# Opening of a fused block: engine orders written out, first block's tokens before the value weights' scale, first x tiles loaded first

## The chip, the cores and the metric

The kernel runs on one core of a Trainium2 chip. The metric is the device time of one execution in microseconds (us); lower is better. The engines are PE (TensorE: matrix products and transpositions), DVE (VectorE), ACT (ScalarE), POOL (GpSimd) and SP (SyncE, which issues nearly all DMAs here). Each works through its own queue in order and waits on semaphores of the others.

## The reference

The block is an attention layer followed by a mixture of 4096 small experts with product keys, each behind a layer norm, for 2048 tokens of 448 features, 16 heads. The change touches only the attention's projections:

```python
def _A_ref(x, wqkv, wo):              # x: layernorm(A_x), (1, 2048, 448)
    qkv = (x @ wqkv).reshape(B, S, 3, H, Dh).transpose(2, 0, 3, 1, 4)
    q, k, v = qkv[0], qkv[1], qkv[2]
    scores = jnp.einsum("bhqd,bhkd->bhqk", q, k) * (Dh ** -0.5)
    p = _softmax(scores, axis=-1)
    o = jnp.einsum("bhqk,bhkd->bhqd", p, v)
    return o.transpose(0, 2, 1, 3).reshape(B, S, D) @ wo
x = A_x
h = x + _A_ref(_layernorm(x), A_wqkv, A_wo)
return h + _B_ref(_layernorm(h), ...)
```

## The kernel before

The program has three parts: the projections to queries, keys and values (`qkv`, the first 154 us), attention woven with preparations of the experts, and the experts. The opening is the start of the first part. It works on blocks of 512 tokens (four blocks, `b`), each of four tiles of 128 tokens (`j`).

Every float32 product is made of three float16 products: an operand is split into a high and a low float16 part (`products`, eleven PE rows for the 448 features: four high x high, four high x low, three low x high; the last 64 features' low part sits in the free half of the fourth high tile, which `lows` patches in with its second instruction).

Weights must be scaled by a power of two first. `Scale` does that: `see` reduces each weight tile to a maximum per partition (DVE, line 141), `spread` reduces these and spreads the result over a 128x128 tile `every` (lines 144 and 145), PE transposes it (line 149), and `set` makes the maximum over all partitions and from it the scale in four small dependent steps (lines 161 to 164). `scaled` then has ACT write the high parts (`wqkh`, `wvh`, line 355) and DVE the low parts (`wqkl`, `wvl`, line 356). `scale_wqk(g)` does it for the key and query weights of head group `g` (two tiles `wqkr`), `scale_wv` for the value weights (two tiles `wr`).

`normed(b)` normalizes a block: statistics per tile (lines 393 and 394), the reciprocal root on POOL (`rsqrt`, lines 109 and 112), the normalization itself into one of two buffers `xn` (line 115), four PE transpositions into one of two PSUM buffers `tr` (line 121), ACT's copy to the high part `XH` (line 96), and DVE's low part `XL` and patch of `XH` (lines 127 and 128).

`keys(0, b)` projects a block to keys (`proj`, PE line 92 into `pq`), squares and copies them on ACT (lines 429 and 431), stores both halves, sums the squares on PE (line 434) and keeps a maximum. `values_of(b)` projects the block's four tiles to values (44 PE rows, line 92) and scales them on ACT (line 416).

`qkv` runs under a scheduler that orders PE, DVE, ACT and SP by itself; only POOL's order is the program's. The code's order there is `scale_wqk(0)`, `normed(0)`, `scale_wv()`, `normed(1)`, and then block by block keys and values. All loads are issued by SP: constants `ct`, two `wqkr`, four tiles of x, two `wr`, then the next x tiles, the next weights and, ahead of need, weights of the later parts.

## Time and profile before

| what | value |
|---|---|
| median of 3 runs | 1644.02 us (1638.12, 1644.02, 1646.05) |
| profiled execution | 1642.62 us, of which the span from first to last instruction is 1640.8 us |
| busy share of the span | PE 95%, DVE 73%, ACT 57%, POOL 22% |
| mean granted PE clock | 0.987 |
| PE waits longest in the first 40 us | 8.2 us for `every`, 6.6 us for `xn` (four times), 2.0 us for the weight scale |

The profile is a record of one execution. The sum of busy times tells which engine is full over the whole span; the windows tell it stage by stage, and the timeline shows each engine's instructions with their start, their length and, in brackets, the idle time before them and what ended it. Rows of equal instructions are merged (x8), so that a row's length is that of the group.

### The profile page before, as it was taken

To read this page: it belongs to the slowest core of one execution; us is meant where nothing else is said; L and a number is where in the kernel's file an instruction comes from. 1 tells how busy PE (TensorE), PEld (TensorE's weight loads), DVE (VectorE), ACT (ScalarE), POOL (GpSimd) and SP (SyncE) were. 2 spreads that over 40 slices of the span, in tenths; PEclk is the share of its full clock that TensorE was granted. 3 is DMA by queue.
4 is the path that set the end of the run, shared out by engine and by line. 5 is a ranking of instruction groups with operands and counts; after the bars stand their busy time and mean duration, and the time that the engine had idled before them with its cause. 6 is when DMAs were issued, how large, how long until landed. Compare 5 with 4: busy or idle time off the path is not lost.

```text
span 1640.8 us, 33316 instructions
## 1 busy us (share of the span) xinstructions
PE 1560.6 (95%) x12585; PEld 678.9 (41%) x12585; DVE 1198.4 (73%) x3875; ACT 931.9 (57%) x1272; POOL 364.7 (22%) x488
## 2 busy tenths in 40 slices
PE   5999999999999998999988998999999999999999
PEld 3444222233333332233325654455545554555444
DVE  7762432645688677765798999959999899779832
ACT  3545778979888887888773443233423344334322
POOL 1241003555204565487524000000000000000000
PEclk9999999999999999999998999999999999999999
DMA  8424965677853475457622434444444533554454
GB/s 281 134 97 129 305 215 190 213 242 253 286 173 96 151 242 180 130 162 235 189 87 78 131 94 148 125 125 144 119 127 138 156 105 108 156 153 129 117 146 129
DMA packets 158881, 263.34 MB, mean 160 GB/s; under 512 B 14336, under 2 KB 90880, under 8 KB 158720
## 3 DMA queue, kind: packets, MB, share of 16 engines
q1 hardware_dynamic: 154496, 259.12, 50.5%
q10 hardware_dynamic: 4224, 2.10, 0.4%
q8 instruction: 98, 1.61, 0.4%
q14 instruction: 63, 0.52, 0.1%
HBM read 211.88 MB, written 49.28 MB: 159 GB/s over the span
## 4 chain that ended last, share of the span: by engine, by line
PE 63%; DVE 27%; DMA 5%; ACT 2%; issue 2%; POOL 1%; SPq 0%; DVEq 0%; POOLq 0%; ACTq 0%
PE acc L1190 14%; PE M L92 12%; PE A L589 10%; PE S L563 9%; PE A L92 7%; PE pq L92 6%; DVE p L969 4%; DVE ti L799 3%; DVE pos L826 2%; DVE G L990 2%; DVE ti L798 2%; ACT P L567 2%; DVE fg L954 2%; DMA raw<-in_uT_dram 2%; PE M L262 1%
## 5 line engine op out<-in xcount | busy, mean ns | idle before, releaser
L567 ACT ACTIVATE P<-S,escale 128x1024 f32<-128x1024 f32 x512 | 534.5, 1131 | 75.9 <-PE S L563 75.9
L1190 PE MATMUL acc<-v,w 128*128 128x448 f16 x1536 | 305.4, 352 | 0.1
L589 PE MATMUL A<-P,V 128*32 128x512 f32 x2048 | 266.0, 609 | 3.7 <-DVE o L594 3.7
L563 PE MATMUL S<-qS,kS 32*128 32x512 f16 x3072 | 240.1, 380 | 7.7 <-ACT P L567 6.0
L1190 PEld LDWEIGHTS <-w 128*128 128x128 f16 x1536 | 148.7, 98 | 141.3 <-ACT w L1164 0.9
L1164 ACT ACTIVATE w<-ring 128x512 f16<-128x512 f32 x128 | 80.5, 630 | 209.7 <-PE acc L1190 109.9
L92 PEld LDWEIGHTS <-u 128*128 128x128 f16 x1408 | 133.7, 98 | 152.5 <-issue 12.3
L969 DVE TENSOR_TENSOR p<-st,iota 128x2048 f16<-128x2048 f16 x128 | 156.0, 1219 | 7.7 <-PE A L996 4.1
L563 PEld LDWEIGHTS <-kS 32*128 32x128 f16 x3072 | 65.8, 92 | 210.6 <-issue 171.7
L92 PE MATMUL A<-XHb,u 128*128 128x512 f16 x568 | 137.8, 386 | 5.1 <-DVE G L990 3.9
L1165 DVE SCALAR_TENSOR_TENSOR w<-w,ring 128x512 f16<-128x512 f16 x128 | 87.2, 687 | 66.2 <-ACT w L1164 66.2
L92 PE MATMUL M<-w,XHb 128*128 128x512 f16 x512 | 127.9, 380 | 4.2 <-DVE ob L580 3.1
L1163 DVE SCALAR_TENSOR_TENSOR ring<-ring,wscale,G 128x512 f32<-128x512 f32 x128 | 92.7, 744 | 34.6 <-ACT ring L1149 34.5
L92 PE MATMUL M<-XHb,u 128*128 128x512 f16 x456 | 112.4, 382 | 0.8 <-DVE G L990 0.8
L1149 ACT ACTIVATE ring<-A,ugelu 128x512 f32<-128x512 f32 x71 | 48.5, 684 | 84.6 <-PE A L92 84.6
L589 PEld LDWEIGHTS A<-P,V 128*32 128x32 f32 x2048 | 45.8, 109 | 119.1 <-issue 108.3
L850 POOL TENSOR_TENSOR sel<-sel,iv 128x256 f16<-128x256 f16 x80 | 54.4, 712 | 171.6 <-DVE sel L846 171.6
L798 DVE MAX8 ti<-fresh 128x8 f32<-128x64 f32 x384 | 80.6, 210 | 16.3 <-ACT fresh L776 16.2
L1149 ACT ACTIVATE ring<-M,ugelu 128x512 f32<-128x512 f32 x57 | 39.2, 688 | 81.7 <-PE M L92 81.5
L799 DVE FIND_INDEX8 ti<-ti,fresh 128x8 uint32<-128x64 f32 x384 | 84.2, 219 | 0.0
L1026 POOL TENSOR_SCALAR raw<-raw,scale 128x512 f32<-128x512 f32 (+1 forms) x64 | 47.3, 740 | 151.8 <-PE M L262 112.2
L954 DVE TENSOR_TENSOR fg<-f,st 128x2048 f16<-128x2048 f16 x64 | 78.0, 1218 | 0.1
(197 smaller groups left out, 2130.4 us busy)
## 6 DMA issues: line engine op xcount, KB each, us to landing
v<-vs SPq DMA_DIRECT2D x128, 336.0 KB, 2.9
u<-us SPq DMA_DIRECT2D x128, 256.0 KB, 2.6
w<-wp SPq DMA_DIRECT2D x56, 512.0 KB, 5.9
kS<-ks SPq DMA_DIRECT2D x64, 256.0 KB, 4.5
V<-vd SPq DMA_DIRECT2D x64, 256.0 KB, 2.8
raw<-in_uT_dram SPq DMA_DIRECT2D x64, 256.0 KB, 5.3
wr<-in_wq_dram SPq DMA_DIRECT2D x32, 448.0 KB, 4.3
raw<-in_v_dram SPq DMA_DIRECT2D x64, 224.0 KB, 5.1
```

Of the source, the lines that this page charges most:

```text
L92: nc.tensor.matmul(ps, l, r, start=i == 0, stop=i == len(pairs) - 1)
L563: nc.tensor.matmul(S[j // 2][:, j % 2], kS[r, a, 128 * (k % 4):128 * (k % 4) + 128], qS[r, c], start=m == 0, stop=m == 2)
L567: nc.scalar.activation(Pt[:, 2 * i:2 * i + 2], S[i], AF.Exp, scale=escale[:, n % 4:n % 4 + 1])
L589: nc.tensor.matmul(O[n][32 * j:32 * j + 32], V[:, k % 4, j], Pt[:, j], start=k == 0, stop=k == NT - 1)
L798: nc.vector.max(t8[:, 4 * i + k], src[:, 64 * k:64 * k + 64])
L799: nc.vector.max_index(i8[:, 4 * i + k], t8[:, 4 * i + k], src[:, 64 * k:64 * k + 64])
L954: nc.vector.tensor_tensor(fg.rearrange("p t k f u -> p t k (f u)"), f1.rearrange("p t f u -> p t (f u)").unsqueeze(2).to_broadcast([128, T ...
L969: newest[0] = nc.vector.tensor_tensor(p1, pairs(0, s, TG, 128), ids(TG, 128), op=OP.is_equal).ins
L1149: nc.scalar.activation(act, p, AF.Gelu_apprx_tanh, scale=ugelu)
L1163: nc.vector.scalar_tensor_tensor(av, av, wscale, of_expert(b, f), op0=OP.mult, op1=OP.mult)
L1165: nc.vector.scalar_tensor_tensor(w[:, 1], w[:, 0], -LS, a, op0=OP.mult, op1=OP.add)
L1190: nc.tensor.matmul(acc[j][:, :D], l, r, start=f == 0 and k == 0, stop=f == 31 and k == 2)
```

## The change

No operation is added or removed. Three things move.

The loads: the first two tiles of x are issued before the constants and the first key and query weights, the other two behind them.

The order of the opening: `scaled` and the two scale functions become generators that stop after each step, `normed` is cut into the methods of `Tokens`, and a new function `opening` calls the steps one by one, with the engines PE, DVE and ACT bound to the order in which they are written. It holds the first weights' scale, all of block 0's normalization, the first key product, the value weights' scale and the key rows' end. The scheduler may still put other work (statistics of later blocks, reductions of later weights) between these steps. `values_of(0)` then comes before `normed(1)`, not behind the keys.

The diff, cut to its core:

```diff
-        nc.sync.dma_start(ct, cst)
+        load_x(0, (0, 1))
+        nc.sync.dma_start(ct, cst)
         fetch_wqk(0)
-        load_x(0)
+        load_x(0, (2, 3))
...
             S.spread()
+            yield
             S.set(S.turned(ps, "tr")[:, 0])
+            yield
             for wr, (hi, low) in zip(raws, parts):
                 nc.scalar.activation(hi, wr, AF.Identity, scale=S.scale)
+                yield
                 nc.vector.scalar_tensor_tensor(low, wr, S.scale, hi, op0=OP.mult, op1=OP.subtract)
+                yield
...
+        class Tokens:
...
+            def stats(self, j, n=1):
+                nc.vector.bn_stats(self.st[:, j], self.xt[:, j])
+                nc.vector.bn_aggr(self.mv[:, j], self.st[:, j])
+                if n:
+                    rsqrt(self.rstd[:, j + 1 - n:j + 1], self.mv[:, j + 1 - n:j + 1, 1], n, XS)
+            def high(self, j):
+                xn = wk.tile([128, D], F32, name="xn")
+                norm(self.xt[:, j], xn, self.mv[:, j, 0:1], self.rstd[:, j:j + 1], nc.vector)
+                self.pt[j] = ps.tile([128, 4, 128], F32, name="tr")
+                turn(self.pt[j], xn)
+                copy(nc.scalar, XH[self.b][:, :, 128 * j:128 * j + 128], self.pt[j])
+            def low(self, j):
+                c = slice(128 * j, 128 * j + 128)
+                lows(XH[self.b][:, :, c], XL[self.b][:, :, c], self.pt.pop(j))
...
+        def opening():
+            wq, wv = scale_wqk(0), scale_wv()
+            T = Tokens(0)
+            nc.scalar.activation(blk, ct[:, C_BLK:C_BLK + 128], AF.Copy)
+            T.stats(0)
+            T.stats(1)
+            next(wq)
+            T.high(0)
+            T.stats(2)
+            next(wq)
+            next(wq)
+            T.high(1)
+            T.stats(3)
+            T.low(0)
+            T.high(2)
+            T.low(1)
+            T.high(3)
+            next(wq)
+            T.low(2)
+            T.low(3)
+            load_x(2)
+            pk = proj(wqks[0][0], 0)
+            for _ in wq:
+                pass
+            next(wv)
+            next(wv)
+            next(wv)
+            keep_keys(0, 0, pk)
+            for _ in wv:
+                pass
         def qkv():
-            scale_wqk(0)
-            normed(0)
-            scale_wv()
-            nc.scalar.activation(blk, ct[:, C_BLK:C_BLK + 128], AF.Copy)
+            with tc.manual_schedule(engines={ET.PE, ET.DVE, ET.Activation}):
+                opening()
             fetch_wqk(1)
+            values_of(0)
             normed(1)
             for b in range(NB):
                 if b in (1, 2):
                     normed(b + 1)
-                keys(0, b)
-                if b < 2:
+                if b:
+                    keys(0, b)
+                if b == 1:
                     values_of(b)
```

What this makes of the engines' queues is seen at three places. Rows are given as line, operation, output and input; `tops` are the maxima of a weight tile, `top` and `floor` the steps to its scale. First DVE, from the end of block 0's low parts to the spread of the value weights' maximum. Before:

```order
L141 TENSOR_REDUCE tops_331<-wr 128x1
L393 BN_STATS st<-xb 128x6
L127 TENSOR_TENSOR XL_206<-tr,XH_202 128x3x128
L128 TENSOR_TENSOR XH_202<-tr,XH_202 64x128
L144 TENSOR_REDUCE top_332<-tops_331 128x1
L127 TENSOR_TENSOR XL_206<-tr,XH_202 128x3x128
L128 TENSOR_TENSOR XH_202<-tr,XH_202 64x128
L145 COPY every<-top_332 128x128
```

Now:

```order
L127 TENSOR_TENSOR XL_206<-tr,XH_202 128x3x128
L128 TENSOR_TENSOR XH_202<-tr,XH_202 64x128
L360 SCALAR_TENSOR_TENSOR wqkl<-wqkr,scale_262,wqkh 128x512
L373 TENSOR_SCALAR escale<-floor_261 128x1
L141 TENSOR_REDUCE tops_346<-wr 128x1 x2
L404 BN_AGGR mv<-st 128x2
L403 BN_STATS st<-xb 128x6
L144 TENSOR_REDUCE top_347<-tops_346 128x1
L403 BN_STATS st<-xb 128x6
L145 COPY every<-top_347 128x128
```

The first of the two value reductions (`tops` from `wr`) stood further up before, at row 18 of DVE's queue, the second ahead of the last two tiles' low parts; now both stand together behind all low parts and the weights' low part.

Second PE, from the end of the first key product to the first value row. Before:

```order
L92 LDWEIGHTS wqkh
L92 MATMUL pq<-XL_206,wqkh 128x512
L121 MATMUL tr<-ct,xn 128x128 x8
L92 LDWEIGHTS XH_202
L92 MATMUL pq<-wvh,XH_202 128x448
```

Now:

```order
L92 LDWEIGHTS wqkh
L92 MATMUL pq<-XL_206,wqkh 128x512
L149 MATMUL tr<-ct,every 128x128
L92 LDWEIGHTS XH_202
L92 MATMUL pq<-wvh,XH_202 128x448
```

Eight transpositions of block 1 stood between the key product and the values; now the spread of the value weights' maximum stands there, which before came in the middle of the key product.

Third PE, where block 0's values end and block 1's keys begin. Now:

```order
L92 LDWEIGHTS XL_206
L92 MATMUL pq<-wvh,XL_206 128x448
L121 MATMUL tr<-ct,xn 128x128 x16
L92 LDWEIGHTS wqkh
L92 MATMUL pq<-XH_203,wqkh 128x512
L121 MATMUL tr<-ct,xn 128x128 x4
```

Before, the same place read:

```order
L92 LDWEIGHTS XL_206
L92 MATMUL pq<-wvh,XL_206 128x448
L121 MATMUL tr<-ct,xn 128x128 x8
L92 LDWEIGHTS wqkh
L92 MATMUL pq<-XH_203,wqkh 128x512
```

All sixteen transpositions of block 1 now stand in one piece behind the values of block 0; before, they were done by then, and the eight shown were the first of block 2.

More of the change, by code (lines that the diff above doesn't have):

```diff
@@ L473, in qkv @@
                 if g < 3:
-                    scale_wqk(g + 1)
+                    for _ in scale_wqk(g + 1):
+                        pass
                 if g < 2:
```

42 lines of the change are left out of this document (18 added, 24 removed).

## The prediction

> **What bounds the kernel now.** I read the page first: the busy digits of the 40 slices, then the chain that ended last.
>
> ```profile
> PE   5999999999999998999988998999999999999999
> DVE  7762432645688677765798999959999899779832
> ...
> PE 63%; DVE 27%; DMA 5%; ACT 2%; issue 2%; POOL 1%; SPq 0%; DVEq 0%; POOLq 0%; ACTq 0%
> ```
>
> A slice is 41 us. PE is at 9 tenths or more nearly everywhere except in the first, and it holds 63% of the chain, so what the change can win lies in that first slice. Windows of 10 us show how much (busy us of PE follow the first comma):
>
> ```profile
> 0.00:10.00 10.00, 0.47 (x1) 0.18 (x1) 4.11 (x13) 1.59 (x2) 1.91 (x18) 1.00 0.77 236
> 10.00:20.00 10.00, 5.37 (x20) 3.67 (x20) 9.79 (x26) 3.61 (x6) 2.24 (x5) 1.00 0.89 295
> 20.00:30.00 10.00, 7.95 (x43) 4.46 (x43) 9.02 (x26) 4.90 (x8) 1.35 (x3) 1.00 0.84 292
> 30.00:40.00 10.00, 8.70 (x50) 4.68 (x49) 8.84 (x23) 4.00 (x8) 2.23 (x3) 1.00 1.01 296
> 50.00:60.00 10.00, 9.91 (x54) 5.22 (x52) 5.97 (x13) 5.16 (x9) 1.16 (x1) 1.00 0.37 117
> ```
>
> PE idles 9.5, 4.6, 2.1 and 1.3 us in the first four windows, 17.5 in all; from 40 us it works without a break, through to 60. DVE is busy 9.8, 9.0 and 8.8 us of the second to fourth: the opening is a DVE stage, and each PE wait in it ends on a DVE result. The timeline gives the head of it (start, length):
>
> ```profile
> 1.28 1.34 SPq L332 DMA_DIRECT2D wqkr<-in_wqk_dram  x2
> 2.66 2.04 SPq L324 DMA_DIRECT2D xb<-in_x_dram  x4
> ...
> 5.78 1.49 DVE L141 TENSOR_REDUCE tops<-wqkr 128x1 f32<-128x512 f32 x2 [5.78 <-DMA wqkr<-in_wqk_dram]
> ...
> 8.18 0.47 PE L149 MATMUL tr<-ct,every 128*128 128x128 f32 x1 [8.18 <-DVE every L145]
> ...
> 10.08 0.51 DVE L115 TENSOR_SCALAR xn<-xb,mv,rstd 128x448 f32<-128x448 f32 x1
> 10.50 0.15 DVE L164 TENSOR_SCALAR scale<-floor 128x1 int32<-128x1 int32 x1
> ...
> 10.64 1.97 PE L121 MATMUL tr<-ct,xn 128*128 128x128 f32 x8 [1.98 <-DVE scale L164]
> ```
>
> The key/query weights (wqkr) land first and their scale is ready at 10.65; the first normalized tile is finished at 10.6, so both arrive together. These eight transpositions take 0.25 us each; the same eight at 24.43 below take 0.13, so PE is still at half rate here, whatever the clock column of the window 10:20 says (1.00). Next, the middle part:
>
> ```profile
> 8.04 1.15 DVE L393 BATCH_NORM_STATS2 st<-xb 128x6 f32<-128x448 f32 x2
> ...
> 11.17 1.08 DVE L141 TENSOR_REDUCE tops<-wr 128x1 f32<-128x896 f32 x1
> 12.16 1.41 DVE L356 SCALAR_TENSOR_TENSOR wqkl<-wqkr,scale,wqkh 128x512 f16<-128x512 f32 x2
> 13.48 0.56 DVE L127 TENSOR_TENSOR XL<-tr,XH 128x384 f16<-128x384 f32 x1
> 14.05 0.29 DVE L128 TENSOR_TENSOR XH<-tr,XH 64x128 f16<-64x128 f32 x1
> 15.26 0.94 DVE L115 TENSOR_SCALAR xn<-xb,mv,rstd 128x448 f32<-128x448 f32 x2
> 18.54 1.86 PE L92 MATMUL pq<-XH,wqkh 128*128 128x512 f16 x4 [0.69 <-ACT XH L96]
> 21.81 0.81 PE L92 MATMUL pq<-XL,wqkh 128*128 128x512 f16 x3
> 22.27 0.12 DVE L164 TENSOR_SCALAR scale<-floor 128x1 int32<-128x1 int32 x1
> 23.15 1.96 ACT L355 ACTIVATE wvh<-wr,scale 128x896 f16<-128x896 f32 x2
> 24.43 1.06 PE L121 MATMUL tr<-ct,xn 128*128 128x128 f32 x8 [1.81 <-DVE xn L115]
> 25.10 1.08 ACT L96 ACTIVATE XH<-tr 128x512 f16<-128x512 f32 x2
> 25.33 0.92 PE L92 MATMUL pq<-wvh,XH 128*128 128x448 f16 x4
> ```
>
> The key product runs from 18.54 to 22.62. The value scale (wr, wvh) is ready at 22.39, because the first value reduction stood in DVE's queue at 11.17, early, in the shadow of loads and scales. PE idles 1.8 us, does eight transpositions of block 1 and starts the values at 25.33. And the end of the opening:
>
> ```profile
> 35.02 0.73 PE L92 MATMUL pq<-wvh,XL 128*128 128x448 f16 x3
> 36.95 1.06 PE L121 MATMUL tr<-ct,xn 128*128 128x128 f32 x8 [1.20 <-DVE xn L115]
> 37.85 1.03 PE L92 MATMUL pq<-XH,wqkh 128*128 128x512 f16 x4
> ...
> 50.41 1.04 PE L121 MATMUL tr<-ct,xn 128*128 128x128 f32 x8
> ```
>
> The values of block 0 end at 35.75, the key product of block 1 starts at 37.85, and at 50.41 the transpositions of block 3 begin. At that last place the changed program has issued exactly the same set of PE instructions as this one, and from there on the orders of the engines agree. So the whole effect can be read as: when does PE reach that place, 50.41 now? PE has no slack behind it, so a shift there is a shift of the end.
>
> **The change, step by step.** No instruction is removed or added; only order and load order change. I walk the new queues with the durations above.
>
> Loads: SP needs 0.5 us per x tile (four in 2.04) and 0.67 per weight tile. Two x tiles ahead put the two weight loads 1.0 us later. The first lands 4.5 us after its issue now (1.28 to 5.78); taking the same, the new landings are about 6.8 and 7.5 and the two reductions (starts 0.7 apart) end at 8.3 instead of 7.2. The x tiles come long before; their statistics are hidden in DVE's wait.
>
> First tile: it stands directly behind the spread of the maximum, at 8.3 + 0.15 + 0.2 = 8.7, against 10.08: 1.4 us won. PE starts 0.5 later, at 9.3.
>
> Weight scale: its PE spread now stands behind four transpositions (4 x 0.25) and takes 0.47: 10.7. Then a reduction of 0.27 and three dependent small steps, which cost 0.19 each back to back:
>
> ```profile
> 61.84 0.15 DVE L163 TENSOR_SCALAR floor<-top 128x1 int32<-128x1 int32 x1
> 62.03 0.15 DVE L164 TENSOR_SCALAR scale<-floor 128x1 int32<-128x1 int32 x1
> ```
>
> So the scale is ready at 11.5, 0.9 later than now.
>
> First block: between the scale and the last patch DVE has one normalization (0.47), two statistics (0.54 each), four low parts (0.57 + 0.30 each), two more normalizations and one low weight part (0.70): 6.8 us, and about 0.3 of waiting for ACT's fourth copy: 18.6. PE does the fourth tile's transpositions at 15.9 to 16.9, ACT copies it in 0.6, and the key product starts at 17.7 (now 18.54). Its eleven rows take 0.43 each until the clock rises. I keep that at about 21.5, where it rises now: end at 22.2, 0.4 us won. That is all that is left of the head start.
>
> Value scale: both value reductions now stand behind all of this. From 18.6: second low weight part 0.7, two reductions of 1.0, two statistics of block 1 and small steps 1.4, then the spread: 22.9 us. Behind the spread come PE's 0.42, 0.27, and, between the small steps, two more statistics and three aggregates: 25.3. **The value scale is 2.9 us later than now** (22.39). What is late next is ACT's first value part, 1.96 / 2 = 0.98: PE starts the values at 26.4, having waited since 22.2, and without block 1's first eight transpositions, which now fill such a wait.
>
> Values: 44 rows of 0.19 (four in 0.92, of which 0.35 is the last one's length), the row of squares 0.33, and 0.3 of waiting: 35.3. Then all sixteen transpositions of block 1 in a row. Eight take 1.06; the third tile needs a normalization and a buffer that are free only after ACT's copy (0.54) and DVE's low part (0.87): PE idles about 1.5, then 0.35 and, before the product that needs the fourth copy, 0.85. The product starts at 40.1, not 37.85: 2.3 late. Eight transpositions of block 2 that are done by 37.85 now are still to come, 1.06, of which 0.3 to 0.7 replaces idle time that follows now. Place 50.41 is reached at about 53.4: **3 us late**.
>
> Moved work that I cost at nothing: the squares and the key copy on ACT, now behind the first value part (they feed a maximum that is complete only after block 3, far behind), and POOL's reciprocal roots, which run while DVE is at the weight reductions or another tile. If that cover went, ACT's two rows would cost about 1.1 us at the 0.54 of a copy. SP's reloads of x are issued as DVE frees the tiles; their statistics are DVE fillers in the value scale's chain, already counted.
>
> Bounds: weight landings 0.8 earlier or later move the place by 0.3 down or 0.8 up by the same walk. The order's own cost is 2.4 to 3.9.
>
> **The clock.** The wait of 22.2 to 26.4, broken by one transposition, is longer than any in this opening after PE speeds up. What does such a wait do? Windows of 1 us elsewhere in the trace; the third number from the end is the granted clock:
>
> ```profile
> 962.00:963.00 1.00, 0.24 (x10) 0.14 (x6) 1.00 (x2) 0.60 (x1) 0.00 (x0) 1.00 0.99 382
> 964.00:965.00 1.00, 0.90 (x34) 0.80 (x31) 1.00 (x2) 0.38 (x1) 0.00 (x0) 0.50 0.99 352
> ...
> 1013.00:1014.00 1.00, 0.00 (x0) 0.00 (x0) 1.00 (x5) 0.17 (x1) 0.00 (x0) 1.00 0.00 0
> 1015.00:1016.00 1.00, 0.94 (x6) 0.66 (x6) 1.00 (x9) 0.88 (x5) 0.00 (x0) 0.50 0.00 0
> 1018.00:1019.00 1.00, 1.00 (x6) 0.54 (x5) 1.00 (x11) 0.22 (x1) 0.00 (x0) 0.91 0.48 188
> ...
> 1015.06 0.58 PE L899 MATMUL M<-ident,sl 128*128 128x128 f16 x4 [5.17 <-ACT st L96]
> ```
>
> After 5.17 idle us PE comes back at 0.50 of its clock and is at full rate again within 1018 to 1019, some 3.4 us on. But it also stood at 0.50 at 964, where it had only thinned out (0.24 busy in the us before 963), not stopped. So I expect a half-rate spell here: value rows at 0.38 instead of 0.19 from 26.4 until somewhere between 28.5 and 32, 30.2 in the middle: 1.9 us, less 0.4 that PE would wait for ACT's second value part anyway: **1.5 us** (bounds 0 and 2.5).
>
> The Trainium skill, TensorE: Matmul & The Clock Gate, section "What's actually happening", puts the fall to half rate behind at least one idle window of about 3.4 us. Read to the letter, the transposition at 22.9 splits this wait into stretches that are too short, and the sum would be 3.0. The rows at 962 to 964, half rate after a window that was only thin, speak for the wider reading, and I follow them.
>
> **Sum.** 3.0 + 1.5 = 4.5 us. Against the profiled execution (span 1640.8, time 1642.62) that is 1647.1; the median of the runs, 1644.02, is 1.4 above that execution, so the forecast is **1648.5**.
>
> **Rivals.**
> - *No half-rate spell.* Order alone: +3.0, 1647. For it: PE stayed at full rate over the 1.8 us before 24.43. Against: this wait is twice as long.
> - *Two spells.* The stretch from 36.4 to 40.1, with 1.06 us of work in it, is as thin as that at 962. A second spell costs another 1.5 to 2, with the wider ends +6 to +9: 1651.
> - *The head start survives (the other side).* If DVE gets the value scale out by 22.4, PE never waits for it and the 1.4 us won at the first tile reach the end: 1642.6. It decides at the value scale: up to 1.5 us later than now the order still gains or breaks even. For it: the first 11 us of DVE hold long waits for loads, and x now comes first. Against: 2.0 us of value reductions stand behind the last patch, where nothing hides them.
> - *Nothing reaches the end.* A later wait that does not depend on this one swallows it: 1644. Against: PE works through the window 50:60 without a break, so nothing else is waited for there that could absorb 3 us.
>
> **How the numbers follow.** One spell 0.40 and none 0.22 make up the forecast (own range 1645 to 1652); two spells 0.17; the other side 0.12; nothing 0.09. Runs of one kernel here lie between 1638 and 1646, so 0.5%, 8.2 us, is about what can be told from no change. The range is 1640 to 1655: from the head start, less 2.6 of scatter, to two spells, plus 4. Slower by over 0.5% needs two spells at their upper end, or the forecast with scatter against it: 0.14. Faster by over 0.5% has no mechanism, as 17.5 idle us cannot fall by half with the loads where they are; scatter leaves 0.03. Within: 0.83.
>
> **What would show it.** First transposition near 9.3; weight scale near 11.5; key product from about 17.7; value scale (L164, second time) near 25.3; first value row near 26.4, with rows of 0.38 behind it and a granted clock below 1 between 24 and 32; sixteen transpositions after the values with about 2.7 us of idle time among them; block 3's transpositions near 55. A value scale before 23.9 us, or PE reaching block 3 before 50, would make the prediction wrong.

## The result, and the profile after

| what | before | after |
|---|---|---|
| median of all runs | 1643.55 us (22 runs, 1638.12 to 1647.30) | 1648.55 us (22 runs, 1644.46 to 1652.72) |
| profiled execution (span) | 1642.62 us (1640.8) | 1648.36 us (1645.3) |
| first transposition of a normalized tile | 10.64 us | 9.02 us |
| value weights' scale ready | 22.39 us | 25.41 us |
| first value row | 25.33 us | 26.54 us |
| block 3's transpositions | 50.41 us | 55.32 us |

The changed kernel takes 1.0032 times as long, 95% interval 1.0024 to 1.0039, which is 3.9 to 6.4 us. On the page, PE's digits of the 40 slices differ from those of before in two slices (the 6th and the 22nd), DVE's in seven, each by one tenth:

```profile
PE   5999989999999998999987998999999999999999
DVE  7763342555689677765798899959999899779832
```

The first slice, where the change is, has PE's old digit: a loss of 5 us does not show at that scale. Windows of 10 us of the changed kernel (PE's busy us stand behind the first comma, the granted clock is the third number from the end):

```profile
0.00:10.00 10.00, 0.98 (x5) 0.93 (x5) 4.40 (x11) 1.59 (x2) 2.48 (x19) 1.00 0.80 236
10.00:20.00 10.00, 5.71 (x19) 2.98 (x18) 8.58 (x22) 3.72 (x6) 1.29 (x3) 1.00 0.91 301
20.00:30.00 10.00, 6.55 (x18) 2.33 (x17) 9.81 (x28) 3.03 (x4) 1.72 (x2) 0.83 0.95 340
30.00:40.00 10.00, 8.40 (x49) 4.70 (x47) 7.71 (x18) 3.60 (x7) 3.41 (x4) 1.00 0.83 245
50.00:60.00 10.00, 9.95 (x56) 5.49 (x55) 4.52 (x12) 4.07 (x7) 1.79 (x3) 1.00 0.59 168
```

PE does 0.5 and 0.3 us more than before in the first two windows, and then only 6.55 in the third, where it did 7.95, and part of it at a lower clock (0.83). The fourth is at 8.40 for 8.70. From 50 us it is full again (9.95 of 10), so that PE has no idle time left there in which it could make the loss good. The steps of the prediction in PE's timeline of the changed kernel (start, length, idle time before it and what ended it):

```profile
9.02 1.12 PE L121 MATMUL tr<-ct,xn 128*128 128x128 f32 x4 [9.02 <-DVE xn L115]
...
17.93 1.86 PE L92 MATMUL pq<-XH,wqkh 128*128 128x512 f16 x4 [0.68 <-ACT XH L96]
...
21.30 1.48 PE L92 MATMUL pq<-XL,wqkh 128*128 128x512 f16 x3
...
26.54 1.28 PE L92 MATMUL pq<-wvh,XH 128*128 128x448 f16 x3 [3.11 <-ACT wvh L358]
...
36.17 0.73 PE L92 MATMUL pq<-wvh,XL 128*128 128x448 f16 x3
36.73 1.04 PE L121 MATMUL tr<-ct,xn 128*128 128x128 f32 x8
39.24 0.63 PE L121 MATMUL tr<-ct,xn 128*128 128x128 f32 x4 [1.47 <-DVE XH L128]
40.13 0.63 PE L121 MATMUL tr<-ct,xn 128*128 128x128 f32 x4 [0.27 <-DVE XH L128]
41.45 0.38 PE L92 MATMUL pq<-XH,wqkh 128*128 128x512 f16 x1 [0.69 <-ACT XH L96]
...
55.32 1.04 PE L121 MATMUL tr<-ct,xn 128*128 128x128 f32 x8
```

The first tile is 1.6 us ahead of before, the key product 0.6, the first value row 1.2 behind, the key product of block 1 3.6 behind (41.45 for 37.85), and block 3's transpositions 4.9 behind. PE's wait of 3.11 us before 26.54 ends on ACT's first value part (`wvh`), and that starts when DVE has the value scale out, in the same kernel:

```profile
11.09 0.15 DVE L164 TENSOR_SCALAR scale<-floor 128x1 int32<-128x1 int32 x1
...
12.57 0.63 DVE L403 BATCH_NORM_STATS2 st<-xb 128x6 f32<-128x448 f32 x1 [0.37 <-DMA xb<-in_x_dram]
...
19.60 2.07 DVE L141 TENSOR_REDUCE tops<-wr 128x1 f32<-128x896 f32 x2
...
25.29 0.12 DVE L164 TENSOR_SCALAR scale<-floor 128x1 int32<-128x1 int32 x1
25.45 1.04 ACT L358 ACTIVATE wvh<-wr,scale 128x896 f16<-128x896 f32 x1 [6.96 <-DVE scale L164]
```

Both value reductions (`tops<-wr`, 2.07 us) stand behind the whole of block 0; the row at 12.57, a statistic that waits for its load, comes up again below. And the clock, in windows of 1 us:

```profile
26.00:27.00 1.00, 0.46 (x2) 0.24 (x2) 1.00 (x3) 1.00 (x3) 0.00 (x0) 0.75 0.97 351
28.00:29.00 1.00, 1.00 (x4) 0.47 (x4) 0.84 (x3) 0.48 (x1) 0.80 (x1) 0.50 1.02 388
29.00:30.00 1.00, 1.00 (x5) 0.38 (x3) 1.00 (x1) 0.00 (x0) 0.92 (x2) 0.54 0.78 303
30.00:31.00 1.00, 1.00 (x7) 0.51 (x6) 1.00 (x2) 0.00 (x0) 0.92 (x2) 1.00 0.86 250
```

Half rate, from 26.50 to 29.91 by windows of 0.1 us: 3.41 us, under the first value rows.

The shift stays to the end of the projections. ACT's small step that closes them (`warm`), in the view of that tile, comes at 142.0 us before and at 146.8 after; from block 3's transpositions to this step it takes 91.5 us in both, and 91.2 to 92.0 in the fourteen profiles of this document. From there to the end the two profiles also take the same (1640.8 - 142.0 = 1498.8 and 1645.3 - 146.8 = 1498.5), but that is chance: in the other twelve this rest takes 1494.3 to 1503.5, with 29 to 56 us of it at half rate. What one execution's opening loses can thus be hidden in its total, and only the many timed runs show it there.

### The profile page after: what moved, and what is told of

It reads as the page before. It is cut to its first block, busy times and chain, and to the rows that moved or that the text cites. A ratio compares the mean times of both kernels' runs of the same rounds, so it can differ in the third digit from the quotient of the medians.

```text
span 1645.3 us, 33316 instructions
## 1 busy us (share of the span) xinstructions
PE 1561.2 (95%) x12585; PEld 677.3 (41%) x12585; DVE 1197.8 (73%) x3875; ACT 931.8 (57%) x1272; POOL 365.5 (22%) x488
## 3 DMA queue, kind: packets, MB, share of 16 engines
q8 instruction: 98, 1.61, 0.4%
## 4 chain that ended last, share of the span: by engine, by line
PE 68%; DVE 22%; DMA 3%; ACT 2%; issue 2%; SPq 0%; POOL 0%; DVEq 0%; ACTq 0%
PE acc L1243 15%; PE M L92 12%; PE A L642 11%; PE S L616 10%; PE A L92 8%; PE pq L92 5%; DVE p L1022 4%; DVE ti L852 2%; DVE G L1043 2%; DVE pos L879 2%; ACT P L620 2%; DVE fg L1007 2%; PE M L262 1%; DMA raw<-in_uT_dram 1%; PE A L1049 1%
```

## The experiments

All are read by the same places. "Half rate" is the time between 23 and 46 us at which the granted clock stands at 0.50; the last two columns are the start of block 3's transpositions in the profiled execution and the ratio of the times to the kernel before.

| kernel | value scale | first value row | half rate, us | block 1's first transposition | block 3's transpositions | ratio (95% interval) |
|---|---|---|---|---|---|---|
| before | 22.39 | 25.33 | none | 24.43 | 50.41 | 1 |
| after | 25.41 | 26.54 | 26.50-29.91 | 36.73 | 55.32 | 1.0032 (1.0024-1.0039) |
| after, a second time | 25.09 | 26.21 | 24.76-31.58, 41.82-45.24 | 37.39 | 56.71 | 1.0027 (1.0015-1.0039) |
| before, new loads alone | 24.59 | 28.36 | 26.11-29.52 | 26.63 | 53.55 | 1.0020 (1.0007-1.0033) |
| after, old loads | 27.67 | 28.80 | 28.95-32.37, 42.61-46.02 | 39.03 | 58.10 | 1.0039 (1.0024-1.0054) |
| after, 13 unread rows | 25.63 | 26.76 | 41.63-45.04 | 35.98 | 57.04 | 1.0039 (1.0025-1.0054) |
| after, 5 unread rows | 25.95 | 27.08 | 28.21-31.63, 41.87-45.28 | 37.35 | 56.71 | one run, 1650.05 us |
| after, value reductions early | 22.94 | 24.74 | 37.89-44.71 | 34.23 | 54.95 | 1.0008 (0.9995-1.0020) |
| after, four PSUM buffers | 26.05 | 27.18 | 26.08-32.91 | 38.54 | 56.36 | 1.0013 (1.0000-1.0026) |
| after, later work held | 22.89 | 24.02 | 24.58-28.00, 38.24-45.06 | 34.28 | 55.48 | one run, 1644.75 us |
| after, block 3 held | 25.67 | 26.80 | 27.31-30.72, 40.96-44.37 | 37.05 | 55.99 | 1.0022 (1.0012-1.0032) |
| both: unread rows, block 3 held | 25.82 | 26.95 | 40.52-43.93 | 36.17 | 55.33 | 1.0023 (1.0009-1.0037) |
| early and block 3 held | 23.24 | 24.85 | none | 34.33 | 52.81 | 1.0010 (0.9996-1.0024) |
| reordered | 22.35 | 23.48 | none | 32.14 | 49.85 | 0.9985 (0.9973-0.9997) |

The two rows of the changed kernel itself are 1.4 us apart in block 3's transpositions. A difference of that size between two single profiles shows nothing alone.

### Which part costs: loads and order apart

The kernel before with the new loads, and the changed kernel with the old ones. In the kernel before:

```diff
+        load_x(0, (0, 1))
         nc.sync.dma_start(ct, cst)
         fetch_wqk(0)
-        load_x(0)
+        load_x(0, (2, 3))
```

> The kernel before with the new load order alone (two tiles of x, the constants, the key/query weights, the other two tiles); the scheduler plans the opening itself. My theory, the loads are not what costs the 4.9 us, the written order is: in this kernel the weights land about 0.8 us later and the weight scale comes later than in the kernel before, at 11.5 to 12.6, but the value reductions stay early, the value scale comes at 23.2 to 24.6 and block 3's transpositions start at 50.8 to 52.6 (50.4 before, 55.3 in the changed kernel). Rival, the load order is the cause: the place is at 54 or later.

And in the changed kernel:

```diff
-        load_x(0, (0, 1))
         nc.sync.dma_start(ct, cst)
         fetch_wqk(0)
-        load_x(0, (2, 3))
+        load_x(0)
```

> The changed kernel with the old load order (constants, key/query weights, four tiles of x). In the written order the statistics of x stand in VectorE's queue ahead of the weight reductions, so the weights, which land at 5.8 and 6.6, must wait for the x tiles near 7.2 and 7.7: my theory expects the first transposition at 10.5 to 11.2, the weight scale at 13 to 13.8, the value scale at 26.8 to 27.7, and block 3's transpositions at 56.8 to 58.2, 1.5 to 3 us later than in the changed kernel. Rival, the new load order is what costs: the place is at 53.5 or earlier.

The place, by loads and order: 50.41 (old, old), 53.55 (new loads alone), 58.10 (new order alone), 55.32 (both). The new loads cost 3.1 us where the scheduler orders, 0.95 more than the upper end that I had given them and 0.45 short of the rival's 54, and win 2.8 where the order is written (1.4 against the changed kernel's second profile). PE's timeline of the kernel before with the new loads:

```profile
9.24 0.48 PE L149 MATMUL tr<-ct,every 128*128 128x128 f32 x1 [9.24 <-DVE every L145]
11.19 1.97 PE L121 MATMUL tr<-ct,xn 128*128 128x128 f32 x8 [1.48 <-DVE top L162]
...
26.63 1.94 PE L121 MATMUL tr<-ct,xn 128*128 128x128 f32 x8 [2.94 <-DVE xn L115]
28.36 1.50 PE L92 MATMUL pq<-wvh,XH 128*128 128x448 f16 x4
```

The weights' maximum is spread 1.06 us later (9.24 for 8.18), the value scale comes 2.2 later, PE waits 2.94 us for block 1's tile, and that wait brings a half-rate window which was not there before. In the changed kernel with the old loads DVE shows the other side:

```profile
7.62 0.63 DVE L402 BATCH_NORM_STATS2 st<-xb 128x6 f32<-128x448 f32 x1 [7.62 <-DMA xb<-in_x_dram]
...
9.11 1.25 DVE L141 TENSOR_REDUCE tops<-wqkr 128x1 f32<-128x512 f32 x2
```

The weights are there first, but the written order asks for x first: the reductions start at 9.11 instead of 6.60. All places of this kernel are at the upper end of what was expected or just above it. By these profiles order and loads belong together: the written order is the costlier half (58.10), and the new loads give a part of it back. The value scale says the same beyond the scatter: 27.67 with the old loads, 25.1 to 26.1 in the seven profiles that keep the new loads and the written order up to there. The timed runs show that the new loads alone cost something (1.0020), but not that they win in the written order: 1.0039 (1.0024 to 1.0054) and 1.0032 overlap.

### The value reductions early

The changed kernel with the reductions back among block 0's tiles, and the value weights' spread and scale ahead of the key product.

```diff
                 S.see(i, wr.rearrange("p t c -> p (t c)"))
+                yield
...
             next(wq)
+            next(wv)
             next(wq)
             T.high(1)
...
             T.low(1)
+            next(wv)
             T.high(3)
+            next(wv)
             next(wq)
             T.low(2)
             T.low(3)
             load_x(2)
+            next(wv)
+            next(wv)
             pk = proj(wqks[0][0], 0)
             for _ in wq:
                 pass
-            next(wv)
-            next(wv)
-            next(wv)
             keep_keys(0, 0, pk)
```

> The changed kernel with the two reductions for the value weights' maximum put back between the statistics and patches of block 0 (the first right after the key weights' scale step, the second ahead of the fourth normalized tile), and with the spread and the scale steps of the value weights ahead of the key product; loads as in the changed kernel. My theory, the place of the value reductions sets the value scale and that the first value row: value scale at 22.4 to 23.2 instead of 25.4, key product 1.5 to 2.4 later (19.4 to 20.3), first value row at 24.0 to 25.0, no half-rate spell, block 3's transpositions at 52.0 to 53.2 instead of 55.3: the time 2 to 3 us less than the changed kernel. Rival, the block 1 transpositions in one piece alone cause the loss: the value scale comes early but the place stays above 54.5.

The value scale (22.94), the first value row (24.74) and the clock up to there came as expected, the key product (20.54) 0.24 above its range: the place of the two reductions, with the spread and the scale steps that moved with them, sets them. Block 3's transpositions did not: 54.95, not 52.0 to 53.2, and above the 54.5 that was to speak for the rival, the sixteen transpositions in one piece. PE's timeline shows where it was lost again:

```profile
34.23 1.04 PE L121 MATMUL tr<-ct,xn 128*128 128x128 f32 x8
37.25 0.63 PE L121 MATMUL tr<-ct,xn 128*128 128x128 f32 x4 [1.99 <-DVE XH L128]
```

Block 1's third tile comes 3.02 us after the first two, 2.51 in the changed kernel, and this thin stretch brings two half-rate windows, 37.89 to 44.71. In ten timed runs the kernel is nevertheless nearly as fast as before: 1.0008 (0.9995 to 1.0020), an interval that does not overlap the changed kernel's (1.0024 to 1.0039). By the times, then, most of the loss does hang on the place of these steps. One execution's half-rate windows need not be another's, as is shown further down.

### Later work held out of the value scale's chain

Statistics of later blocks and reductions of later weights (the same edit at `see` and `spread`) may not stand ahead of the value scale's last step; `SV` is the value weights' `Scale`.

```diff
-            nc.vector.tensor_scalar(self.scale.bitcast(I32), self.floor.bitcast(I32), -1.0, float((2 * 127 + TOP) << 23),
-                                    op0=OP.mult, op1=OP.add)
+            self.last = nc.vector.tensor_scalar(self.scale.bitcast(I32), self.floor.bitcast(I32), -1.0, float((2 * 127 + TOP) << 23),
+                                                op0=OP.mult, op1=OP.add).ins
...
-                nc.vector.bn_stats(self.st[:, j], self.xt[:, j])
-                nc.vector.bn_aggr(self.mv[:, j], self.st[:, j])
+                with tc.issue_after(SV.last) if hasattr(SV, "last") else nullcontext():
+                    nc.vector.bn_stats(self.st[:, j], self.xt[:, j])
+                    nc.vector.bn_aggr(self.mv[:, j], self.st[:, j])
```

> The changed kernel with VectorE's statistics of the later blocks and the reductions of later weights held back until the value weights' scale is out; same work, other place. My theory counts these as 1.4 us and more in the chain of the value scale: the scale comes at 24.0 to 24.6 instead of 25.4 and the first value row near 25.4; but block 1's statistics then come late, its first transposition waits for them, and block 3's transpositions start later than in the changed kernel, at 55.5 to 57. Rival, the fillers cost nothing because they lie in the wait between the dependent small steps: value scale within 0.3 of 25.4.

The scale comes at 22.89, 2.5 us earlier, more than the 0.8 to 1.4 expected. From the start of the value reductions to the scale it takes 3.86 us (19.03 to 22.89) and not 5.81 (19.60 to 25.41), so that the fillers in the chain cost 1.95 us, about as much as the two reductions (2.07). The rest was won ahead of it, by another filler: in the changed kernel the statistics of block 1's first tile stand between those of block 0's fourth tile and their closing step, and wait there for their load until 12.57 (0.37 us idle). That wait was 1.12 us with four PSUM buffers and none in the changed kernel's second execution, and is a part of the value scale's scatter. In DVE's timeline of this kernel the small steps start 0.33, 0.18 and 0.19 after each other, where it was up to 0.8 with statistics between them:

```profile
22.04 0.29 DVE L162 TENSOR_REDUCE top<-tr 128x1 f32<-128x128 f32 x1 [0.49 <-PE tr L150]
22.37 0.15 DVE L163 TENSOR_SCALAR top<-top 128x1 f32<-128x1 f32 x1
22.55 0.15 DVE L164 TENSOR_SCALAR floor<-top 128x1 int32<-128x1 int32 x1
22.74 0.15 DVE L165 TENSOR_SCALAR scale<-floor 128x1 int32<-128x1 int32 x1
```

As expected the place does not follow (55.48), but not for the reason given: block 1's first transposition did not wait for its statistics (its tile was normalized from 30.37 on, and the transposition stands directly behind the values at 34.28). Its third and fourth tiles came later, after waits of 1.61 and 0.80 us for 1.47 and 0.27, and with two half-rate windows behind the values it takes 21.2 us from block 1's first transposition to block 3's, instead of 18.59.

### Four PSUM buffers for transposed tiles

```diff
-        ps = c0.enter_context(tc.tile_pool(name="ps0", bufs=2, space=PSUM))
+        ps = c0.enter_context(tc.tile_pool(name="ps0", bufs=4, space=PSUM))
```

> The changed kernel with four instead of two PSUM buffers for transposed tiles; order of the opening unchanged. My theory, the sixteen transpositions of block 1 in one piece lose time because the third tile waits for a buffer: everything up to 36.5 us stays (value scale 25.4, first value row 26.5, spell 26.3 to 29.7), the idle time of TensorE between the first and the last transposition of block 1 falls from about 1.7 us to under 0.9, and block 3's transpositions start at 53.8 to 54.4 instead of 55.3. Rival, the third tile waits for its normalization in VectorE's queue and not for the buffer: the place moves by less than 0.4 us.

PE's timeline shows block 1's sixteen transpositions nearly closed up:

```profile
38.54 1.04 PE L121 MATMUL tr<-ct,xn 128*128 128x128 f32 x8
39.75 1.09 PE L121 MATMUL tr<-ct,xn 128*128 128x128 f32 x8 [0.17 <-DVE xn L115]
```

The third tile comes 1.21 us after the first, not 2.51: it was the buffer. From block 1's first transposition to block 3's it takes 17.82 us instead of 18.59. The place itself is at 56.36, above the range, because this execution had its value scale 0.6 later (the load of block 1's first tile, awaited until 13.28) and two half-rate windows (26.08 to 32.91) under the value rows. The timed runs, 1.0013, are better than that one profile.

### The half-rate window by itself

Thirteen products more, which nobody reads, in PE's wait ahead of the values; in the second kernel five. (The window's ends in the expectation, 26.26 and 29.7, were read too early; by windows of 0.1 us they are 26.50 and 29.91.)

```diff
             next(wv)
             next(wv)
+            dead = ps.tile([128, 512], F32, name="dead", bufs=1)
+            for i in range(13):
+                nc.tensor.matmul(dead, wqks[0][0][0][:, 0], XH[0][:, 0], start=True, stop=True)
             next(wv)
```

> The changed kernel with 13 matrix products more, whose result nobody reads, put on TensorE between the transposition of the value weights' maximum and the first value row; nothing else is moved. My theory: the one window at half rate (26.26 to 29.7 us in the changed kernel) comes from the thin stretch 22.8 to 26.5; rows that fill it keep the granted clock at 1.00 from 24 to 32 us, the value rows take 0.19 us each from the start, value scale (25.4) and first value row (26.5) stay where they are, and block 3's transpositions start at 53.6 to 54.0 instead of 55.3; the time falls by about 1.5 us. Rival A, the half rate costs nothing because the value rows wait for ScalarE's and VectorE's parts of the weights anyway: clock 1.00, but the place stays at 55.0 to 55.5. Rival B, the half rate has a cause other than PE's idleness: the clock falls at 26.3 as before and the place stays at 55.3.

> The same with 5 unread products instead of 13 (about 1.1 us of the 3.5 us wait are filled). If the spell needs a stretch with no work at all, five rows prevent it as thirteen do (clock 1.00 from 24 to 32, block 3's transpositions near 53.8); if a thin stretch is enough, as I read the rows at 962 to 964 us of the kernel before, the clock still falls to 0.50 near 26.3 and the place stays near 55.3. I expect the second, without much certainty.

Thirteen rows keep the clock at 1.00 from 24 to 32 us, as expected, and the values take 9.22 us from their first row to block 1's first transposition (26.76 to 35.98), where they took 10.19 with one half-rate window and 11.18 with two. So one window costs 1.0 us there, by these three profiles. But the place is at 57.04, beyond what any theory gave, and the time did not fall (1.0039 for 1.0032). PE and, below it, DVE of this kernel:

```profile
35.98 1.04 PE L121 MATMUL tr<-ct,xn 128*128 128x128 f32 x8
40.49 0.63 PE L121 MATMUL tr<-ct,xn 128*128 128x128 f32 x4 [3.48 <-DVE XH L128]
```

```profile
37.59 1.15 DVE L403 BATCH_NORM_STATS2 st<-xb 128x6 f32<-128x448 f32 x2 [2.59 <-DMA xb<-in_x_dram]
38.66 0.92 DVE L115 TENSOR_SCALAR xn<-xb,mv,rstd 128x448 f32<-128x448 f32 x2
```

Two statistics (line 403; those of block 3, whose x tiles are loaded into block 1's buffer once its first two tiles are normalized) stand in DVE's queue ahead of block 1's third normalized tile and wait for their load until 37.59. The same two rows waited until 35.58 in the changed kernel, where the half-rate value rows hid them. The load itself was issued at nearly the same time in both, 32.81 there and 33.03 here, so that it was its landing that differed:

```profile
35.58 1.25 DVE L403 BATCH_NORM_STATS2 st<-xb 128x6 f32<-128x448 f32 x2 [0.81 <-DMA xb<-in_x_dram]
37.37 0.95 DVE L115 TENSOR_SCALAR xn<-xb,mv,rstd 128x448 f32<-128x448 f32 x2 [0.54 <-PE tr L121]
```

With five rows (they end at 25.04, the value rows start at 27.08) PE is busy for some 1.4 of the 3.41 us before 28.21, and the clock falls all the same: a thin stretch is enough, as the rows near 962 us said.

### A new theory: block 3's statistics hold block 1

```diff
-                T.stats(j, 4 * (j == 3))
+                with tc.issue_after(patched[1]) if b == 3 else nullcontext():
+                    T.stats(j, 4 * (j == 3))
```

Here `patched[1]` is the last patch of block 1. The edit was made in the changed kernel alone, with the thirteen unread rows, and with the value reductions early. Beside them the changed kernel ran once more, without an edit.

> The changed kernel with one move: block 3's statistics, whose first two stood in VectorE's queue ahead of block 1's third normalized tile and waited there for their load (until 35.58 us in the changed kernel, until 37.59 with thirteen unread rows), are queued behind block 1's last patch. My new theory: the value rows and these statistics end together in the changed kernel (36.7 and 36.8), so one taken away alone leaves the other: value scale 25.2 to 25.9, one half-rate window, and block 3's transpositions 28.2 to 28.9 us after the first value row (28.78 in the changed kernel): less than 0.6 us won. Rival, the statistics alone hold block 1: 27.3 to 28.0 after the first value row.

> Both together: the thirteen unread rows that keep the clock up, and block 3's statistics behind block 1's last patch. My new theory: only both set block 1 free. The value rows run at 0.19 us each and end near 36, the third tile follows without the 3.48 us wait that the unread rows alone had, and block 3's transpositions come 27.1 to 27.9 us after the first value row (28.78 in the changed kernel, 30.28 with the unread rows alone), no second half-rate window near 41; the time 0.5 to 3 us below that with the unread rows alone. Rival, block 1 is bound by something else, GpSimd's reciprocal roots or the buffers: 28.7 or more after the first value row.

> The experiment with the value reductions early, and block 3's statistics behind block 1's last patch. There the value scale was ready at 22.94 and the first value row stood at 24.74, but the third tile of block 1 waited 1.99 us and a half-rate spell from 37.9 to 44.7 us took what was won. New theory: with the statistics away the third tile waits 1.4 us or less; block 3's transpositions start at 51.8 to 53.4, 27.1 to 28.5 us after the first value row (30.21 without the move), and the spell near 38 to 44 is shorter or away. Rival, the statistics do not matter there since they did not wait for a load: 54.5 or later.

> The changed kernel a second time, without an edit, to see how far its profiled landmarks scatter. I expect the value scale at 25.2 to 25.9, one half-rate window that begins between 26 and 28.5, and block 3's transpositions at 55.0 to 56.8.

With the statistics held, block 1's third tile follows its first after the same 2.51 us in all three kernels (4.51 with unread rows alone, 3.02 with the early reductions alone); PE's rows of the second and the third of these kernels:

```profile
36.17 1.04 PE L121 MATMUL tr<-ct,xn 128*128 128x128 f32 x8
38.68 0.63 PE L121 MATMUL tr<-ct,xn 128*128 128x128 f32 x4 [1.47 <-DVE XH L128]
```

```profile
34.33 1.04 PE L121 MATMUL tr<-ct,xn 128*128 128x128 f32 x8
36.84 0.63 PE L121 MATMUL tr<-ct,xn 128*128 128x128 f32 x4 [1.47 <-DVE XH L128]
...
52.81 1.04 PE L121 MATMUL tr<-ct,xn 128*128 128x128 f32 x8
```

So the theory on the 3.48 and 1.99 us waits holds. Held alone, the move wins nothing in the changed kernel, as expected, though its 29.19 us from the first value row to the place lie above the 28.9 given, for a second half-rate window. With the unread rows the distance is 28.38, not 27.1 to 27.9: the values run at full rate, and then the 1.47 us wait among block 1's transpositions brings a half-rate window of its own (40.52 to 43.93), which I had said would go. Only the third kernel came in its range (52.81; 27.96), without any window. Against the unread rows alone, the times of the second (1.0023 for 1.0039) point the same way, but the intervals overlap. The times of the third are no better than with the early reductions alone (1.0010 and 1.0008), though its profiled place is 2.1 us earlier: what holding block 3 is worth over many executions is not shown.

The changed kernel's second execution had the value scale at 25.09, earlier than expected, and three half-rate windows instead of one. Windows of 1 us of it:

```profile
24.00:25.00 1.00, 0.00 (x0) 0.00 (x0) 1.00 (x7) 0.00 (x0) 0.00 (x0) 0.88 0.97 376
28.00:29.00 1.00, 1.00 (x4) 0.44 (x3) 1.00 (x2) 0.16 (x1) 1.00 (x1) 0.50 1.01 402
31.00:32.00 1.00, 1.00 (x5) 0.49 (x4) 0.15 (x3) 0.00 (x0) 0.92 (x2) 0.71 0.75 262
```

Its place is at 56.71, 1.4 behind the first execution, though its first value row came 0.3 earlier. The number of half-rate windows is a matter of the execution; that PE gives cause for them is a matter of the order.

### A version made from the reasons

The value reductions early, block 1's statistics and POOL's roots written directly behind the value scale, its four tiles behind the values' low parts (the scheduler then puts them among the value rows), the query weights' low part last, four PSUM buffers.

```diff
+            T1 = Tokens(1)
...
             pk = proj(wqks[0][0], 0)
-            for _ in wq:
-                pass
+            T1.stats(0, 0)
+            T1.stats(1, 0)
             next(wv)
             next(wv)
             next(wv)
+            T1.stats(2, 0)
+            T1.stats(3, 4)
             keep_keys(0, 0, pk)
             for _ in wv:
                 pass
+            T1.high(0)
...
+            T1.low(3)
+            for _ in wq:
+                pass
+            return T1
...
-            with tc.manual_schedule(engines={ET.PE, ET.DVE, ET.Activation}):
+            with tc.manual_schedule(engines={ET.PE, ET.DVE, ET.Activation, ET.Pool}):
```

> A version made from the reasons: the changed kernel's loads and head, the value reductions early as in the experiment on them, the statistics of block 1 and GpSimd's reciprocal roots written out directly behind the value scale, the query weights' low part last, block 1's four transposed tiles written behind the values' low parts so that they fall among the value rows, and four PSUM buffers for transposed tiles. My theory: value scale at 21.7 to 23, first value row at 23.3 to 24.5, no half-rate spell, block 3's transpositions at 48.2 to 50.2 (50.4 before, 55.3 in the changed kernel), time 0.5 to 2.5 us below the kernel before. Rival, the opening is bound by VectorE's total work and no order beats the kernel before: the place is at 50.4 or later.

It is faster than both: 0.9985 of the kernel before (0.9973 to 0.9997; 12 runs, median 1640.84 us beside 1642.74), by 0.5 to 4.4 us. Five things were moved at once, and the kernel before was not run with four PSUM buffers, which alone brought the changed kernel from 1.0032 to 1.0013 with intervals that overlap by little: whether the order or the buffers put this version below the kernel before is not shown. PE's timeline:

```profile
9.45 1.12 PE L121 MATMUL tr<-ct,xn 128*128 128x128 f32 x4 [9.45 <-DVE xn L115]
...
23.48 1.67 PE L92 MATMUL pq<-wvh,XH 128*128 128x448 f16 x8 [0.59 <-ACT wvh L359]
...
32.14 1.06 PE L121 MATMUL tr<-ct,xn 128*128 128x128 f32 x8 [1.37 <-DVE xn L115]
...
49.85 1.06 PE L121 MATMUL tr<-ct,xn 128*128 128x128 f32 x8
```

The head start of the first tile (9.45 for 10.64) now reaches the value rows (23.48 for 25.33), at full clock, but of its 1.9 us only 0.6 are left at block 3: block 1's tiles waited 1.37 us for their normalization, which stood behind POOL's reciprocal root, begun only at 29.26.

## Why the prediction was right, and where it was not

**The head of the opening.** First transposition 9.3, measured 9.02; weight scale 11.5, measured 11.24; key product from 17.7, measured 17.93. Its end, 22.2, was 22.78: PE's rows took 0.43 up to there, so the clock rose later than the 21.5 which I had kept. The x tiles do not all come long before they are needed, as the walk says: block 1's first was awaited until 12.57. And not each wait of PE in the kernel before ends on DVE: the prediction's own row at 18.54 waited 0.69 us for ACT's copy. Neither moves the sum by more than 0.4 us. The later clock cost nothing, since PE waited for the value scale anyway.

**The value scale.** 25.3 for 25.41, first value row 26.4 for 26.54, and the cause, both value reductions and later work behind block 0's last patch, is shown: with the reductions early the scale came at 22.94, with the later work held at 22.89, and the changed kernel's opening gave 25.1 to 26.1 in seven profiles.

**The half-rate window.** It came where it was expected, 26.50 to 29.91. Its price was mis-sized: 1.5 us in the sum, 0.97 measured (10.19 less 9.22). At half rate 3.4 us lose 1.7, not the 1.9 taken, and full-rate rows had to wait 0.7 us for the values' low parts on DVE (seen with the unread rows), not 0.4 for ACT's second value part.

**The value rows and block 1.** Without the window the values take 9.22 us up to block 1's first transposition; my row count gave 8.7 (from 26.4 to 35.1: the values' end of 35.3 less the 0.17 by which the first transposition overlaps the last row), too short by 0.5. The waits among the sixteen transpositions, 1.5, 0.35 and 0.85, were 1.47, 0.27 and 0.69. From the first of them to block 3's, 18.3 had been counted, 18.59 were measured.

**The sum.** Place 54.9, measured 55.32: +0.1 at the first value row, +0.5 in the value rows, -0.5 for the clock, +0.3 behind, which is 0.4. The two larger errors cancelled. The place carried over to the end of the projections, as said: 4.9 there, 4.8 at their end; that the span then shows 4.5 is chance, as its rest scatters by 9 us. How close the numbers came is luck as well: the changed kernel's second execution had the place at 56.71, and the forecast, 1648.5, meets the median of 1648.55 because the medians moved by 5.0 us, 0.5 more than the 4.5 forecast, while the 1644.02 of three runs that it was added to lay 0.5 above the median of 22. The direction, the path over the value scale and the size of about 5 us were right for the reasons given.

**What the sum hid.** It treated the window as a fixed term, and the loads as a small one (0.3 down, 0.8 up; alone, in the kernel before, they moved the place by 3.1). The second execution of the same kernel had three windows, so the rival of two spells, with its stretch behind the values, was not another outcome beside the forecast but belongs to the same kernel: in seven of the nine further kernels that keep the changed kernel's opening in the main a window fell between 37 and 46 us. And the terms do not add singly: the clock's 1.0 us, taken away alone, came back as a wait for block 3's statistics and a later window. The prediction named that stretch but not the statistics, which no step of it mentions.

**The other rivals.** "No half-rate spell" is refuted for the changed kernel by its clock rows, "nothing reaches the end" by the timed runs and the 146.8 us. "The head start survives" put the decision at the value scale, not more than 1.5 us later than before. That condition alone is not enough: with the scale at 22.94 the place was still 54.95, and with block 3 held 52.81. Only the version with block 1's tiles among the value rows got below the kernel before, and it moved other things too.

**What stays open.** Why the load of block 3's first tiles ended at 35.58 in one execution and at 37.59 in another. Three kernels (early reductions, four buffers, later work held) are faster in their timed runs than their profiled places say. For two of the profiled executions the difference lies behind the opening: with four buffers the rest from `warm` on took 1494.3 us, with the later work held 1495.8, where the kernel before took 1498.8. For the medians it stays open, as one profile of each was taken. What block 1's transpositions in one piece cost by themselves was not measured apart.

## What to carry to other kernels

An order written out by hand is to be followed to the first place at which both programs have issued the same work: a head start at the first tile is worth nothing if the operation that ends the next wait has moved behind it in another engine's queue. Work that the program needs much later (statistics, maxima) is not free as a filler; in a chain of small dependent steps it cost 1.95 us here, and in front of a block's next tile it made that block wait for a load. A thin stretch on PE is paid twice here, once as idle time and once in the clock (0.97 us for a window under the value rows), and whether it is paid in a given execution is partly chance, so a place in one profile is to be compared over more than one execution.

## What the hardware showed that I had not expected

Within one execution the granted clock changes only at points 3.41 us apart: 24.76, 31.58, 41.82 and 45.24 in the changed kernel's second execution are 2, 3 and 1 such steps from each other. The points lie elsewhere in the next execution (26.50 and 29.91 in the first). The fall came after a step in which PE was busy for 0.3 us (before 26.50) and also after one with about 1.4 (five unread rows, before 28.21); after one with 2.0 (24.76 to 28.17 in the second execution, PE at work from 26.21) the half rate stayed for another step. Work of 1.68 us in a step came out both ways: the full rate stayed from 40.15 in the changed kernel, and fell at 40.96 with block 3 held. The start fits the steps: the rows of the changed kernel's key product took 0.43 us each, twice their later time, up to 22.78, and the trace's clock records begin at 23.09, one step before 26.50. Ahead of that the granted clock's column reads 1.00 only because nothing is recorded there.

POOL and DVE held each other up. In the changed kernel DVE's first value low part, begun at 28.89 while POOL's low half of the keys (`fl`, 1.16 us from 28.20) still ran, took 1.41 us, the second 1.14. POOL's reciprocal roots of four tiles, beside these low parts, were slow in their turn:

```profile
29.44 0.92 POOL L109 TENSOR_SCALAR rstd<-mv 128x4 f32<-128x4 f32 x1
30.44 1.80 POOL L112 TENSOR_TENSOR rstd<-rstd,lnpow 128x4 f32<-128x4 f32 x1
```

In the kernel before, where neither ran beside the low parts, the same two rows took 0.20 and 1.02 us, and the low parts 1.14 each. All fourteen profiles agree: the first low part took 1.40 to 1.67 us in the eleven in which it began under `fl`, and 1.12 to 1.15 in the other three. With the later work held, `fl` ran beside the low parts and the roots did not: the first low part took 1.67, the roots 0.20 and 1.01. So DVE's loss went with `fl`, POOL's with the low parts; no experiment was made for it.
